# Whole-array matmuls at the end, a selector normalise for the last groups, and group one's K/Q weights first: a transformer block on one core

## The chip, the cores and the metric

One core of a Trainium2 chip. The metric is device time in microseconds (us) of one execution. A profile gives the span from the first to the last instruction, about 2 us less than the time.

## The reference, cut to what matters

```python
B, S, D, H, F = 1, 2048, 640, 32, 1728          # head size 20
def _A_ref(x, wqkv, wo):
    q, k, v = ...                                # x @ wqkv, 32 heads
    scores = einsum("bhqd,bhkd->bhqk", q, k) * Dh ** -0.5
    return (softmax(scores) @ v).reshape(B, S, D) @ wo
def _B_ref(x, w_gate, w_up, w_down):
    return ((x @ w_gate) * (x @ w_up)) @ w_down
h  = x + _A_ref(layernorm(x), wqkv, wo)
h2 = h + _B_ref(layernorm(h), w_gate, w_up, w_down)
```

## The kernel before

It is a program that schedules itself while it is built: it models the engines, chooses at each step what the matmul engine does next, and emits the instructions in that order. On the chip the order is fixed. Queries are cut into six stages of 512, 512, 384, 256, 256 and 128 rows; heads into eight groups of four. One *bank* is 128 keys by 512 scores of one head; there are 2048. ScalarE (ACT) takes the exponential of most banks, two or three per instruction; VectorE (DVE) makes about 310 of them with integer arithmetic. Everything else (projections, output product, layer norm, gate, up, down) is background between the score matmuls, and the background of the last two stages runs on after the last attention sum.

Names in the profile's lines: A and m are banks of scores (m serves background products too), E their exponentials, acc the attention sums, b the banks of background products after the last sum. 128\*32 is a weight tile of 128 rows and 32 columns, and the next pair gives the moving operand.

The parts that the change touches. Background products, as four tiles of 32 columns, so that they run side by side:

```python
    def columns(ps, lhsT, rhs, start, stop, n, width=P):
        for i in range((width + 31) // 32):
            w = min(32, width - 32 * i)
            mm(ps[32 * i:32 * i + w, 0:n], lhsT[:, 32 * i:32 * i + w], rhs, start, stop)
```

The normalise: each head's sum of exponentials is one row of the accumulator. Rows go to memory and back as columns, get a reciprocal, and are broadcast through DRAM:

```python
        free = en.add("DVE", ..., lambda: nc.vector.tensor_copy(a[:, 0:w], bank[:, 0:w]), 0.5)
        e = dma(lambda: nc.sync.dma_start(s_[:, 0:m], a[DH:P:32, 0:w]...), [free])
        e = en.add("DVE", ..., lambda: nc.vector.reciprocal(r_[:, 0:m], s_[:, 0:m]), 1.5)
        e = dma(lambda: nc.sync.dma_start(d[:, 0:w]..., r_[:, 0:m]), [e])
        e = dma(bcast, [e], ...)                                  # b <- d, 32 times each row
        e = en.add("DVE", ..., lambda: nc.vector.tensor_tensor(OnT[g], a, b, ALU.mult), 1)
```

First loads and what group one waits for; when VectorE may take a small bank; when background of a stage may start:

```python
    load_x(0)
    e_qk0 = [None, load_w(D, D + 160)]
    e_qk0[0] = load_w(0, 160)
    ...                                                           # then x1, V, the rest of K, of Q, of V
        ws = ([e_k, e_qk0[1]] if b == 1 else [e_q, e_qk0[0]]) if g == 1 else [e_qk0[b]]
    ...
                    ok = fr and self.late() <= LAG                # LAG = 100
    ...
                    g.since = g.due = a + (b - a) * SPREAD * (i + 1) / len(groups)   # SPREAD = 1.2
```

The softmax here doesn't subtract the row's maximum and nothing guards it: scores larger than these inputs give would overflow.

## Time and profile before

| | before |
|---|---|
| time, median of 3 (lowest to highest); a fourth run makes it 885.91 below | 885.79 us (883.98 to 886.77) |
| span of the profiled run | 883.0 us |
| matmul engine / VectorE / ScalarE busy | 832.6 / 754.5 / 804.4 us |
| exponentials from / to | 17.7 / 834.8 us |
| last attention sum starts | 835.62 us, 47.4 us before the end |

The lines behind it stand in the prediction. Read the last two rows of the table as the skeleton: the time is the start of the exponentials, plus their work and their holes, plus what comes after the last sum.

### The profile page before, as it was taken

The page shows a single profiled execution, that of the slowest core. Times are in us where ns is not written, and L with a number is a line of the kernel's source. Part 1 is how long each engine was busy: PE and PEld are TensorE (multiplying, and loading weights), DVE is VectorE, ACT ScalarE, POOL GpSimd, SP SyncE. Part 2 cuts the span into 40 slices and gives each one's busy share as a digit, 9 for nine tenths or more (in the row PEclk, how much of TensorE's full clock was granted, in tenths as well). Part 3 has the DMA queues.
Part 4 walks back from the last instruction along what each step waited for, and adds up shares of the span by engine and source line. Part 5 has one row for each costly group of instructions (what it writes and reads, how often), then busy time and mean ns, then how long its engine had stood idle before and what let it go on. Part 6 is the DMA issues. An engine that isn't in the chain of part 4 may idle for free. (4 is left out here: it accounts for less than half of the span.)

```text
span 883.0 us, 36981 instructions
## 1 busy us (share of the span) xinstructions
PE 832.6 (94%) x16596; PEld 367.6 (42%) x16596; DVE 754.5 (85%) x1608; ACT 804.4 (91%) x780; POOL 20.8 (2%) x32
## 2 busy tenths in 40 slices
PE   6999999999999999999999999999999999999995
PEld 2444342232334322222344433344444445565774
DVE  4654886999899999999999999989989997998652
ACT  3699989999999999999999999999999999998801
POOL 2020000000000000000000000000000000000000
PEclk9999999999999999999999999999999999999999
DMA  6131212212230233211310233161034311274100
GB/s 206 39 102 29 82 56 63 84 40 79 64 89 22 67 96 90 53 41 36 67 38 28 50 79 72 27 146 34 23 90 97 66 26 31 67 154 77 23 16 19
DMA packets 132950, 56.62 MB, mean 64 GB/s; under 512 B 103096, under 2 KB 130744, under 8 KB 132792
## 3 DMA queue, kind: packets, MB, share of 16 engines
q1 hardware_dynamic: 132792, 54.27, 24.5%
q8 instruction: 129, 2.11, 1.0%
q14 instruction: 29, 0.24, 0.1%
HBM read 45.89 MB, written 8.09 MB: 61 GB/s over the span
## 5 line engine op out<-in xcount | busy, mean ns | idle before, releaser
L740 ACT ACTIVATE E<-A 128x1536 bf16<-128x1536 f32 (+1 forms) x758 | 795.4, 1183 | 21.1 <-PE A L429 12.4
L429 PE MATMUL A<-qT,kT 32*128 32x256 bf16 (+3 forms) x3024 | 296.9, 299 | 22.8 <-ACT E L740 18.6
L429 PEld LDWEIGHTS <-kT 32*128 32x128 bf16 (+1 forms) x3768 | 101.5, 92 | 256.6 <-issue 216.0
L429 PE MATMUL acc<-E,Vx 128*32 128x256 bf16 (+3 forms) x2808 | 190.1, 304 | 4.7 <-ACT E L740 3.0
L754 DVE TENSOR_SCALAR i<-m 128x512 int16<-128x512 f32 x185 | 125.9, 684 | 11.8 <-PE m L429 10.5
L429 PEld LDWEIGHTS <-Vx 128*32 128x32 bf16 x3328 | 69.5, 95 | 102.5 <-issue 94.0
L784 DVE TENSOR_TENSOR fr<-hl,fr 128x1024 bf16<-128x1024 bf16 x157 | 107.0, 682 | 2.0
L787 DVE TENSOR_TENSOR ED<-i,fr 128x1024 int16<-128x1024 int16 x157 | 106.4, 678 | 1.3
L754 DVE TENSOR_SCALAR i<-A 128x512 int16<-128x512 f32 x128 | 87.7, 685 | 11.4 <-PE A L429 9.5
L429 PE MATMUL m<-lnT,Wr 128*32 128x512 bf16 (+7 forms) x1200 | 74.9, 347 | 2.2 <-DVE lnT L1016 0.8
L429 PE MATMUL m<-qT,kT 32*128 32x256 bf16 (+3 forms) x304 | 71.6, 297 | 0.0
L429 PE MATMUL m<-Wd,hh 128*32 128x320 bf16 (+1 forms) x1456 | 71.0, 301 | 0.2 <-DVE i L754 0.2
L429 PE MATMUL m<-ln2T,wg 128*32 128x512 bf16 (+2 forms) x980 | 70.0, 348 | 0.8 <-DVE i L754 0.8
L429 PE MATMUL m<-ln2T,wu 128*32 128x512 bf16 (+2 forms) x980 | 68.7, 348 | 1.3 <-DVE i L754 1.3
L429 PE MATMUL acc<-zt 128*32 128x512 bf16 (+3 forms) x992 | 67.2, 341 | 0.0
L781 DVE TENSOR_SCALAR hl<-fr 128x1024 bf16<-128x1024 int16 x157 | 65.4, 417 | 1.5
L778 DVE TENSOR_SCALAR fr<-i 128x1024 int16<-128x1024 int16 x157 | 64.4, 414 | 1.3
L429 PEld LDWEIGHTS <-hh 128*32 128x32 bf16 (+1 forms) x1792 | 42.9, 96 | 25.8 <-issue 16.4
L429 PE MATMUL m<-shared,On 128*32 128x320 bf16 x1024 | 49.0, 301 | 0.1
L1406 DVE TENSOR_TENSOR hh<-gs,m 128x512 bf16<-128x512 bf16 (+3 forms) x66 | 36.0, 545 | 9.4 <-PE m L429 5.0
L1395 DVE CAST gs<-m 128x512 bf16<-128x512 f32 (+5 forms) x62 | 35.1, 567 | 7.0 <-PE m L429 6.3
L429 PEld LDWEIGHTS <-Wr 128*32 128x32 bf16 (+1 forms) x1200 | 27.6, 96 | 27.2 <-issue 18.1
(71 smaller groups left out, 541.4 us busy)
## 6 DMA issues: line engine op xcount, KB each, us to landing
wg<-in_B_w_gate_dram SPq DMA_DIRECT2D x47, 160.0 KB
wu<-in_B_w_up_dram SPq DMA_DIRECT2D x47, 160.0 KB
rb<-rd SPq DMA_DIRECT2D x16, 256.0 KB
kT<-kq SPq DMA_DIRECT2D x24, 128.0 KB
kq<-stg SPq DMA_DIRECT2D x24, 120.0 KB
out_dram<-ot SPq DMA_DIRECT2D x16, 160.0 KB
shared<-in_A_x_dram SPq DMA_DIRECT2D x14, 160.0 KB
Wd<-in_B_w_down_dram SPq DMA_DIRECT2D x13, 160.0 KB
```

What stands on the lines that cost most here:

```text
L429: nc.tensor.matmul(out_, lhsT=lhsT, rhs=rhs, start=start, stop=stop)
L740: apart(readers, nc.scalar.activation(E[:, 0:size, :], src[:, 0:size, :], ACT.Exp, scale=LN2_ / UNIT))
L754: apart(readers, nc.vector.tensor_scalar(it[:, pos, :], bank.ap, BIAS, 0.0, ALU.add, ALU.max))
L778: nc.vector.tensor_scalar(f[:, 0:n, :], it[:, 0:n, :], 127, None, ALU.bitwise_and)
L781: nc.vector.tensor_scalar(h[:, 0:n, :], f[:, 0:n, :], QR, QK, ALU.subtract, ALU.mult)
L784: nc.vector.tensor_tensor(fb[:, 0:n, :], h[:, 0:n, :], f[:, 0:n, :], ALU.mult)
L787: nc.vector.tensor_tensor(e16[:, 0:n, :], it[:, 0:n, :], fb[:, 0:n, :], ALU.add)
L1395: r = en.add("DVE", dve_ns(w), [e, was], lambda: nc.vector.tensor_copy(gs[0:M, 0:w], ps[0:M, 0:w]), 1)
L1406: r = en.add("DVE", dve_ns(w), [e, ce, was], lambda: nc.vector.tensor_tensor(hh[0:M, 0:w], gs[0:M, 0:w], ps[0:M, 0:w], ALU.mult), 1)
```

## The change

Its intent: fill the hole in the exponentials near 30 us; shorten the end with fewer, wider matmuls; and take the memory round trip out of the last normalises. New scheduling constants came with it.

```diff
+QK0 = 2 * HP * DH + PADR                       # 172 columns
-    e_qk0 = [None, load_w(D, D + 160)]
-    e_qk0[0] = load_w(0, 160)
+    e_qk0 = [None, load_w(D, D + QK0)]
+    e_qk0[0] = load_w(0, QK0)
-        ws = ([e_k, e_qk0[1]] if b == 1 else [e_q, e_qk0[0]]) if g == 1 else [e_qk0[b]]
+        ws = [e_qk0[b]]
@@ whole-array steps once attention is done
+    def shape(self):
+        return "F" if self.att.done() else "C"
     def columns(ps, lhsT, rhs, start, stop, n, width=P):
+        if pe.mode == "F":
+            mm(ps[0:width, 0:n], lhsT[:, 0:width], rhs, start, stop)
+            return
@@ selector normalise (the last group of stage 4, the last two of stage 5)
+        if g >= G - FAST.get(p, 0):
+            spread(p, g, free, a, b, spots)
+            return free
+    def spread(p, g, free, a, b, spots):
+        ...  # matmul of a with a 0/1 selector puts each head's sum on its 32 rows,
+        ...  # then b = reciprocal(ps), OnT[g] = a * b
@@ constants
+LNP = (1.2, 1.2, 1.2, 1.2, 0, 0)
+WP = (1, 1, 1, 1, 0, 0)                        # priorities: stage 4 now like stage 5
-SPREAD = 1.2
+SPREAD = (1.0, 1.0, 0.9, 0.8)
-LAG = 100
+M_END = 1800
-                    ok = fr and self.late() <= LAG
+                    ok = fr and self.flat < M_END
```

(Cut: the same choice of shape in transposes and filler matmuls, the making of the selector, arguments passed along.)

More of the change, by code (lines that the diff above doesn't have):

```diff
@@ L46 @@
 RES = 5
+FAST_LAST = 2
+FAST_PREV = 1
+LNP = (1.2, 1.2, 1.2, 1.2, 0, 0)
+WP = (1, 1, 1, 1, 0, 0)
 INF = float("inf")
@@ L255, in act @@
             last = g.at == len(g.steps) - 1
-            self.charge(s, dur, "C", dur * 2.4, deps, [g.ev] if last else [])
+            self.charge(s, dur, self.shape(), dur * 2.4, deps, [g.ev] if last else [])
             fn(g.bank.ap, g.at == 0, g.at == len(g.steps) - 1)
@@ L270, in next @@
             if known([self.zeros]) <= t and sum(w for x, w in self.recent if x > t - TICK) < ENOUGH:
-                need = FILL + SWITCH + (SWITCH if self.mode != "C" else 0.0)
+                need = FILL + SWITCH + (SWITCH if self.mode != self.shape() else 0.0)
                 if t + need <= max(latest, s) + 20.0 and t < INF:
@@ L287, in fill @@
         n = bank.shape[1]
-        self.charge(s, n / 2.4 + 3.0, "C", float(n), deps, [])
+        self.charge(s, n / 2.4 + 3.0, self.shape(), float(n), deps, [])
         self.filler(bank, new)
@@ L388 @@
     kap4 = keep.tile([P, HP], F32, name="kap4")
+    sel = keep.tile([P, P], F32, name="sel")
     kT = tiles(keep, G, [P, S], BF16, "kT")
@@ L866, in filler @@
         for i in range(HP):
+            if pe.mode == "F":
+                mm(bank, zt[:, 0:P], zt[:, 0:bank.shape[1]], new, new)
+                break
             mm(bank[32 * i:32 * i + 32, :], zt[:, 0:32], zt[:, 0:bank.shape[1]], new, new)
@@ L880 @@
     wo_done = {}
+    FAST = {LASTP: FAST_LAST, LASTP - 1: FAST_PREV}
     def normalise(p, g, ev):
@@ L916, in normalise, with evac, step @@
         return free
+    def spread(p, g, free, a, b, spots):
+        w = WIDTHS[p]
+        def evac(ps, e):
+            r = en.add("DVE", dve_ns(6.5 * w), [e], lambda: nc.vector.reciprocal(b[:, 0:w], ps[:, 0:w]), 0)
+            q = en.add("DVE", dve_ns(w), [r, Later(lambda: wo_done.get(p - 1))], lambda: nc.vector.tensor_tensor(
+                OnT[g][:, 0:w], a[:, 0:w], b[:, 0:w], ALU.mult), 0)
+            for x in spots:
+                rb_free[x] = q
+            on_ev[p, g] = q
+            return r
+        def step(ps, first, last):
+            columns(ps, sel, a[:, 0:w], first, last, w)
+        for x in spots:
+            rb_free[x] = Ev()
+        pe.groups.insert(0, Group([free, e_sel], [(4 * pe_ns(w), step, [])], evac, f"N{p}{g}"))
+        if g == (G - 1 if p < LASTP else 3):
+            stages.append(p)
     stages = []
@@ L1005, in fn @@
                 pt = ps.bitcast(BF16)
+                if pe.mode == "F":
+                    nc.tensor.transpose(pt[:, c * P:(c + 1) * P], src[:, c * P:(c + 1) * P], ident[:])
+                    return
                 for i in range(4):
@@ L1046, in load_w @@
     def load_w(a, b, after=None):
-        n = (b - a) * D * 2 * (2 if b - a <= 160 else 1)
+        n = (b - a) * D * 2 * (2 if b - a <= QK0 else 1)
         fn = lambda: nc.sync.dma_start(Wr[:, :, a:b], wv[:, :, a:b])
@@ L1064, with one_row @@
     e_kap = en.add("DVE", 80.0, [e_kap], lambda: nc.vector.tensor_reduce(kap[:], kap4[:], mybir.AxisListType.X, ALU.add), 0)
+    e_sel = en.add("POOL", 200.0, [], lambda: nc.gpsimd.memset(sel[:], 1.0), 4)
+    for slope in (1, -1):
+        def one_row(slope=slope):
+            view = sel[:].rearrange("p (h e) -> p h e", e=32)
+            nc.gpsimd.affine_select(out=view, in_=view, compare_op=ALU.is_ge, fill=0.0, base=-slope * DH,
+                                    pattern=[[-32 * slope, HP], [0, 32]], channel_multiplier=slope)
+        e_sel = en.add("POOL", 300.0, [e_sel], one_row, 4)
     e_half = en.add("POOL", 100.0, [], lambda: nc.gpsimd.memset(half[:], 0.5), 0)
@@ L1074 @@
     e_v0 = load_w(2 * D, 2 * D + HD)
-    e_k = load_w(D + 160, 2 * D)
-    e_q = load_w(160, D)
+    e_k = load_w(D + QK0, 2 * D)
+    e_q = load_w(QK0, D)
     e_v1 = load_w(2 * D + HD, 3 * D)
@@ L1338, in evac @@
                     r = en.add("DVE", dve_ns(HD), [e, ex], lambda: nc.vector.tensor_tensor(
-                        hr[:, hsl], ps[:, 0:HD], hr[:, hsl], ALU.add), 1 if not last else 0)
+                        hr[:, hsl], ps[:, 0:HD], hr[:, hsl], ALU.add), WP[p])
                     hv[hf].t2 = r
@@ L1355, in second_stage @@
             evs = layer_norm([hrow[hn(i)] for i in idx], [Max(hev[i]) for i in idx], outs,
-                             [fr.get(("ln", i % 2)) for i in idx], 1.2 if not last else 0)
+                             [fr.get(("ln", i % 2)) for i in idx], LNP[p])
             for i, e in zip(idx, evs):
@@ L1446, in more @@
                 for i, g in enumerate(groups):
-                    g.since = g.due = a + (b - a) * SPREAD * (i + 1) / len(groups)
+                    g.since = g.due = a + (b - a) * SPREAD[p] * (i + 1) / len(groups)
             pe.groups += groups
```

## The prediction

> **What bounds the kernel now.** I read the page's busy shares first, then the busy time by stretches, then the two places that stood out: the opening (in order of time) and the end (chain of waits, then in order of time).
>
> ```profile
> PE 832.6 (94%) x16596; PEld 367.6 (42%) x16596; DVE 754.5 (85%) x1608; ACT 804.4 (91%) x780; POOL 20.8 (2%) x32
> ...
> L740 ACT ACTIVATE E<-A 128x1024 bf16<-128x1024 f32 x539 | 529.5, 1061 | 10.4 <-PE A L429 9.8 <-PE m L429 0.3
> L740 ACT ACTIVATE E<-A 128x1536 bf16<-128x1536 f32 x219 | 325.1, 1485 | 10.7 <-PE m L429 6.7 <-PE A L429 2.6 <-PE acc L429 1.1
> ```
>
> ScalarE does nothing but attention exponentials, 539×2 + 219×3 = 1735 banks of 512 columns; the other 313 of 2048 banks go to VectorE in five instructions each pair.
>
> ```profile
> 20.00:30.00 10.00, 9.80 (x163) 4.13 (x158) 3.46 (x13) 6.27 (x7) 1.01 (x1) 1.00 0.04 5
> 30.00:40.00 10.00, 9.62 (x230) 4.87 (x233) 6.03 (x15) 5.28 (x6) 0.00 (x0) 1.00 0.24 77
> ...
> 200.00:300.00 100.00, 95.28 (x1544) 36.13 (x1542) 92.92 (x199) 100.00 (x99) 1.43 (x2) 1.00 0.22 60
> ...
> 860.00:870.00 10.00, 6.18 (x402) 5.66 (x401) 2.84 (x10) 2.13 (x8) 0.00 (x0) 1.00 0.07 21
> ```
>
> Columns are PE, weight loads, DVE, ACT. From 200 to 700 us ACT is full: there only its work counts. So three terms set the time: how early the exponentials run without a hole, how much of them ACT has, and what is left after the last one (834.8 us). The hole in the opening:
>
> ```profile
> 28.00 1.25 PE L429 MATMUL m<-lnT,Wr 128*32 128x512 bf16 x20
> ...
> 29.31 0.59 ACT L1154 CAST kT<-m 128x512 bf16<-128x512 f32 x1 [0.73 <-PE m L429]
> ...
> 34.72 15.70 ACT L740 ACTIVATE E<-A 128x1024 bf16<-128x1024 f32 x17 [4.83 <-PE A L429]
> ```
>
> Head group one's K projection runs only at 28.00 and its Q later, because their weights ride in the big loads; the eight exponentials of group zero are over at 28.6 and ACT has 6.1 us with 0.59 us of work. The end:
>
> ```profile
> 861.61 1.22 PE b L429 x86
> 862.83 1.57 issue
> 864.40 0.40 PE b L429 x14
> 864.80 0.56 PE m L429 x40
> 865.36 1.01 PE b L429 x74
> 866.37 1.51 issue
> 867.87 0.85 PE b L429 x46
> ...
> 869.84 1.51 issue
> 871.36 2.96 PE b L429 x128
> 874.31 0.80 issue
> ```
>
> Between the stalls stand exactly 128 matmuls (14+40+74), 256 instructions with their weight loads. With one more at 845.74 (1.04 us) they cost 6.43 us in which PE waited for nothing visible. Also there, the normalise of the very last group goes through memory and back:
>
> ```profile
> 836.08 0.29 DVE L896 COPY accS<-acc 128x128 f32<-128x128 f32 x1
> ...
> 842.79 0.54 SPq L903 DMA_DIRECT2D rb<-rd  x1
> ...
> 849.41 0.28 DVE L909 TENSOR_TENSOR On<-accS,rb 128x128 bf16<-128x128 f32 x1
> 850.97 2.02 PEld L429 LDWEIGHTS <-On 128*32 128x32 bf16 x64
> ```
>
> 13.6 us from sums to quotient; the last stage's first product starts at 850.97.
>
> **What the Trainium skill says.** "Runtime: NRT & Kernel Launch", section Instruction fetch mechanics: an engine's instructions come through a FIFO refilled in blocks of 256, and crossing a block is mostly hidden. The trace agrees on 256 and disagrees on hidden: with 128-column matmuls one block lasts 1.97 us of work (864.40 to 866.37) and the next comes 3.47 us after the last. "TensorE: Matmul & The Clock Gate", section Back-to-back issue gap, gives about 81 ns for a pair of weight load and 128-column matmul, against about 56 ns without the load; here four 32-column tiles of 128 columns take 0.56 us per ten, 56 ns, with 4×32 weight columns loaded behind them, and 256 columns take 1.09/10 = 109 ns. No 128x128 weight load is in this trace. "TensorEngine Tiling (Array Packing)", section Restrictions, says column tiling disables fast weight load, so whole tiles should not load slower than now; no line shows it yet.
>
> **The change part by part.** I compared the instruction order of both kernels on every engine; counts below are from there, durations from the rows named.
>
> *First weights.* The first K and Q loads widen from 160 to 172 columns and then hold all of group one. Its two projections move ahead of the value projections, with exponentials 9 to 16 no longer behind the large loads. Removed: the hole of 6.1−0.6 = 5.5 us. Added: 40 matmuls of 512 columns earlier, at the opening's slow rate (40 in 4.46 us), replacing 16 filler matmuls: some 2.5 us in front of exponentials that were PE-paced anyway (1.6 us apart, 1.02 us long), part of it hidden. The next gate, the second chunk's layer norm, was ready about 31 us and its K projection about 36, just when exponential 17 will be due. Net −4.5 us, between −2 and −6.
>
> *Scheduling constants.* VectorE banks drop from 313 to 303: the order shows 118 instead of 128 taken from ACT's own tiles and only one from the small banks after bank 1800. ACT then runs 530 of two banks, 228 of three, one of one. By the row at 34.72 a two-bank one costs 15.70/17 = 0.924 us; with 795.4 us busy in all (page, group one), a three-bank one is (795.4−539×0.924)/219 = 1.36 us. After: 530×0.924+228×1.36+0.5 = 800 us, +4.4 us on the bounding engine. Against it: after 34.72 ACT idles 800.1−787.4 = 12.7 us, 5 of them after 750, where the waits name PE's small banks (m) most, which VectorE now leaves alone late. I take −2 us back, 0 to −6.
>
> *Whole-array matmuls after the last attention sum.* The stages after 835.9 have 103 steps of 256 columns, 56+28 of 320, 16 of 320 for the output projection and 145 of 128 with the transposes; the order has nearly the same steps (102) left, so no work moves. Instructions there fall to a quarter, about 840 of 3300: at 3.47 us per 256 this is 11.4 us of fetching for over 30 us of work, so the 6.4 us of stalls go. PE from 835.84 to 879.37 is 43.5 us; less 6.4 leaves 37.1. If weight loads show at 128 columns, 145 steps cost up to 81−56 = 25 ns more, 3.6 us; I take 10 ns, 1.5 us, 0.5 us for the wider ones. A new wait for the last gate-times-up results before the down projection may cost 1 us, as the fetch stalls hid it until now. Net −4 us, 0 to −7.
>
> *Selector normalise.* Three groups (last of the next-to-last stage, two of the last) replace three transfers by one f32 matmul and a full-width reciprocal. From rows of 242 ns at 16 columns and 167 at 4, a column costs 6.25 ns: about 0.94 us at 128, 1.74 at 256. The quotient comes some 3 us after the last sum instead of 13.6. But PE had work meanwhile (840 to 850: 8.96 of 10 busy) and only 0.95 us near 859.65 waited for the last stage's norm. Worth 1 us at most directly; call it −0.5 and the slack that lets whole-array steps follow each other. VectorE sheds 10 banks at 0.685 + (0.683+0.679+0.418+0.415)/2 = 1.78 us, far more than the 3.6 us of reciprocals.
>
> Sum: −4.5 + 4.4 − 2 − 4 − 0.5 = −6.6 us. I add −1.5 us because the parts' favourable sides are longer (the idle time of ACT in the middle is open to repair), giving 885.8 − 8.1, about 877.7 us, 0.9% less.
>
> **Rivals.** First, that the whole-array loads do not hide: each of about 320 steps then adds some 53 ns of load, 17 us, and the stage loses 10 instead of gaining 4; the time would be about 892. Against: column-tiled steps already load 128 columns per 56 ns unseen, and row-tiled loads of 128 columns start 12 ns apart. For: all of them go to different parts of the array, a whole one does not. Second, that ACT's 10 more banks eat the opening's gain and the idle time stays: −0.1 from both together, and 881 remains from the tail. Third, that the opening's hole only moves, to the wait for the second chunk's projections, as PE is 98% busy between 20 and 30: gain 1 us, about 881. Fourth, everything works: −6, +4.4, −6, −7, −1, about 870. For it: the idle time of ACT after 750 has one kind of cause.
>
> **Range and chances.** 870 to 884 covers the fourth rival and both mild ones, not the first. Over 2% faster means below 868.1, more than all favourable ends together: 0.06. Over 2% slower needs 903, beyond even the first rival: 0.01. Within 2%: 0.93.
>
> **What would show it.** Opening: group one's K copy on ACT right after its first exponential, no 4.83 us wait, the 17th exponential near 37 instead of 42. Middle: ACT busy about 4 us more; the last attention sum between 829 and 836. End: no issue stalls of 1.5 us in the chain, steps of 128 columns at 56 to 81 ns and of 256 at about 109 (more than 130 would mean that loads show and I am wrong there), the last quotient 3 us after its sum, and about 42 us instead of 47 from last sum to end. If the last sum comes earlier than 829, I have mis-sized the scheduling constants; if later than 836, the second or third rival holds.

## The result and the profile after

877.17 us (median of 4, 876.99 to 879.09) against 885.91: ratio 0.991, 95% interval 0.989 to 0.993. A ratio here is the mean time of one kernel's fast runs over that of the other's fast runs of the same rounds, so it is not quite the ratio of the medians.

The page and the exponentials of the kernel after:

```profile
PE 832.1 (95%) x15633; PEld 369.9 (42%) x15633; DVE 738.0 (84%) x1578; ACT 808.1 (92%) x781; POOL 21.0 (2%) x35
...
L753 ACT ACTIVATE E<-A 128x1024 bf16<-128x1024 f32 x530 | 526.7, 1074 | 14.7 <-PE A L439 13.9 <-ACT E L753 0.3
L753 ACT ACTIVATE E<-A 128x1536 bf16<-128x1536 f32 x228 | 341.9, 1500 | 3.4 <-PE A L439 2.5 <-PE acc L439 0.3 <-ACT E L753 0.2
```

ScalarE is busy 3.7 us more; 4.4 were worked out from the order. The opening of the kernel after, in order of time:

```profile
24.62 8.55 ACT L753 ACTIVATE E<-A 128x1024 bf16<-128x1024 f32 x9 [0.27 <-PE A L439]
34.60 11.11 ACT L753 ACTIVATE E<-A 128x1024 bf16<-128x1024 f32 x12 [1.42 <-PE A L439]
...
53.60 6.65 ACT L753 ACTIVATE E<-A 128x1024 bf16<-128x1024 f32 x7 [2.70 <-PE A L439]
...
115.97 7.38 ACT L753 ACTIVATE E<-A 128x1024 bf16<-128x1024 f32 x7 [4.10 <-PE A L439]
```

The 4.83 us hole is gone and the 17th exponential starts at 34.60, where it was near 42 before (34.72 plus eight at 0.924). But new waits for scores stand at 53.60 and 115.97. Busy time by stretches, before:

```profile
45.00:100.00 55.00, 54.10 (x1113) 23.20 (x1105) 29.59 (x76) 52.21 (x56) 5.37 (x2) 1.00 0.25 67
100.00:140.00 40.00, 38.88 (x646) 16.15 (x646) 37.11 (x75) 36.17 (x35) 0.00 (x0) 1.00 0.21 64
```

and after (columns: PE, weight loads, DVE, ACT, POOL):

```profile
45.00:100.00 55.00, 53.31 (x1133) 23.66 (x1135) 28.64 (x70) 49.61 (x52) 5.37 (x2) 1.00 0.25 65
100.00:140.00 40.00, 37.75 (x643) 15.96 (x639) 26.22 (x51) 34.42 (x33) 0.00 (x0) 1.00 0.25 75
```

From 45 to 140 us ScalarE does 4.4 us less and VectorE 11.8 us less than before. I counted the banks whose exponential has started by a time (instructions started in the trace, times the banks of each in the order):

| banks begun by | 45 us | 100 us | 140 us | 200 us | 700 us |
|---|---|---|---|---|---|
| before | 40 | 159 | 253 | 409 | 1718 |
| after | 56 | 167 | 252 | 407 | 1717 |

The lead of 16 banks is spent by 140 us. The last attention sum starts at 834.40, only 1.2 us earlier than before, and 0.9 us of that is a first exponential at 16.77 instead of 17.70. The rest of the gain is in the end, which shrinks from 47.4 to 40.7 us:

```profile
834.85 0.29 DVE L914 COPY accS<-acc 128x128 f32<-128x128 f32 x1
...
835.50 0.39 PE L439 MATMUL b<-accS,sel 128*128 128x128 f32 x2
...
836.12 0.95 DVE L944 RECIPROCAL rb<-b 128x128 f32<-128x128 f32 x1
...
837.26 0.28 DVE L945 TENSOR_TENSOR On<-accS,rb 128x128 bf16<-128x128 f32 x1
...
837.91 1.25 PE L439 MATMUL m<-shared,On 128*128 128x320 bf16 x8
...
859.86 1.00 PE L439 MATMUL b<-ln2T,qT 128*128 128x128 bf16 x15
...
860.70 0.44 PE L439 MATMUL m<-ln2T,qT 128*128 128x128 bf16 x5
```

The quotient is there 2.7 us after the copy of its sum (13.6 before). Fifteen whole-array steps of 128 columns take 860.70 − 859.86 = 0.84 us, 56 ns each, the pace of the column tiles; those of 256 take 109 ns (15 from 835.73 to 837.37). No line of the matmul engine after the last sum waits on "issue" for longer than 0.3 us.

So the total came out as predicted while its parts did not: the opening brought no gain that lasted, and the end brought more. The experiments take the parts one by one.

### The profile page after: what moved, and what is told of

It reads as the page before. It is cut to its first block, busy times and chain, and to the rows that moved or that the text cites. A ratio compares the mean times of both kernels' runs of the same rounds, so it can differ in the third digit from the quotient of the medians.

```text
span 875.1 us, 35020 instructions
## 1 busy us (share of the span) xinstructions
PE 832.1 (95%) x15633; PEld 369.9 (42%) x15633; DVE 738.0 (84%) x1578; ACT 808.1 (92%) x781; POOL 21.0 (2%) x35
## 4 chain that ended last, share of the span: by engine, by line
ACT 46%; PE 36%; DVE 13%; issue 4%; DMA 0%; DVEq 0%; ACTq 0%
ACT E L753 46%; PE m L439 16%; PE A L439 10%; PE acc L439 7%; DVE i L767 4%; PE b L439 3%; DVE fr L797 1%; DVE ED L800 1%; DVE fr L791 1%; DVE hl L794 1%; PE m L1052 1%; DVE gs L1448 1%; DVE hh L1459 1%; DVE accS L914 0%; DVE st L1024 0%
## 5 line engine op out<-in xcount | busy, mean ns | idle before, releaser
L797 DVE TENSOR_TENSOR fr<-hl,fr 128x1024 bf16<-128x1024 bf16 (+1 forms) x152 | 103.7, 682 | 1.6
L800 DVE TENSOR_TENSOR ED<-i,fr 128x1024 int16<-128x1024 int16 (+1 forms) x152 | 103.2, 679 | 1.2
L767 DVE TENSOR_SCALAR i<-A 128x512 int16<-128x512 f32 x118 | 81.0, 687 | 12.7 <-PE A L439 10.0
L439 PE MATMUL m<-Wd,hh 128*32 128x320 bf16 (+1 forms) x1484 | 77.3, 301 | 0.1
L439 PE MATMUL acc<-zt 128*32 128x512 bf16 (+3 forms) x1028 | 72.3, 353 | 0.0
L794 DVE TENSOR_SCALAR hl<-fr 128x1024 bf16<-128x1024 int16 (+1 forms) x152 | 63.7, 419 | 1.3
L791 DVE TENSOR_SCALAR fr<-i 128x1024 int16<-128x1024 int16 (+1 forms) x152 | 62.1, 416 | 0.7
L439 PEld LDWEIGHTS <-hh 128*32 128x32 bf16 (+2 forms) x1540 | 41.9, 96 | 26.9 <-issue 15.1
L439 PE MATMUL m<-shared,On 128*32 128x320 bf16 (+1 forms) x968 | 47.6, 301 | 1.2 <-DVE i L767 0.8
L1459 DVE TENSOR_TENSOR hh<-gs,m 128x512 bf16<-128x512 bf16 (+4 forms) x68 | 36.9, 542 | 6.6 <-PE m L439 3.1
```

The costliest lines, as they stand in the source:

```text
L439: nc.tensor.matmul(out_, lhsT=lhsT, rhs=rhs, start=start, stop=stop)
L767: apart(readers, nc.vector.tensor_scalar(it[:, pos, :], bank.ap, BIAS, 0.0, ALU.add, ALU.max))
L791: nc.vector.tensor_scalar(f[:, 0:n, :], it[:, 0:n, :], 127, None, ALU.bitwise_and)
L794: nc.vector.tensor_scalar(h[:, 0:n, :], f[:, 0:n, :], QR, QK, ALU.subtract, ALU.mult)
L797: nc.vector.tensor_tensor(fb[:, 0:n, :], h[:, 0:n, :], f[:, 0:n, :], ALU.mult)
L800: nc.vector.tensor_tensor(e16[:, 0:n, :], it[:, 0:n, :], fb[:, 0:n, :], ALU.add)
```

## The experiments

The change has four parts: *first* (wider first loads), *whole* (whole-array steps after the last sum), *norm* (selector normalise), *const* (constants). Undoing all four in the changed kernel gives the order of the kernel before on PE, ACT, DVE and the DMA queue, instruction for instruction, so they are complete (the trace of half late below, in which all four are undone, agrees for ACT, DVE and the DMA queue). All results below were correct. Every kernel is within 2% of the kernel before, so what is said rests on the 95% intervals. "Left" is the number of 256-column steps after the last sum, in the order; ten of them are half as wide (64 columns) and count as one each. The prediction and the expectations divide the matmuls of column-tiled kernels by four, so their numbers for these (103, 98, 76, 66) are five lower than here.

| kernel | median us | ratio to before (95%) | last sum starts | end after it | left | banks on DVE |
|---|---|---|---|---|---|---|
| before | 885.8 | | 835.6 | 47.4 | 108 | 313 |
| changed | 877.2 | 0.991 (0.989 to 0.993) | 834.4 | 40.7 | 102 | 303 |
| whole only | 879.2 | 0.992 (0.990 to 0.995) | 834.1 | 40.5 | 108 | 313 |
| first only | 888.4 | 1.002 (1.000 to 1.005) | 843.0 | 46.0 | 103 | 310 |
| norm only | 885.5 | 0.999 (0.997 to 1.001) | 841.0 | 42.7 | 81 | 310 |
| const only | 881.0 | 0.994 (0.991 to 0.997) | 835.8 | 45.3 | 71 | 310 |
| changed without first | 875.0 | 0.987 (0.984 to 0.991) | 835.8 | 34.3 | 57 | 310 |
| changed without whole | 880.8 | 0.995 (0.992 to 0.998) | 833.5 | 45.9 | 102 | 303 |
| changed without norm | 878.1 | 0.992 (0.989 to 0.994) | 837.3 | 40.3 | 107 | 303 |

Single executions of one kernel spread over up to 9 us (the kernel before: 880.0 to 889.1), so the two columns from one trace each explain, and the ratios decide.

### One part alone

**whole only** (edit: first, norm and const undone).

> The kernel before with only the whole-array steps after the last attention sum. Everything up to the last sum is the same order of instructions, so the last exponential should end at 834.8 us again, within 1. If the gain of the end is instruction fetch (the four or five stalls of 1 to 1.6 us, 6.4 us in all, gone because the instructions fall to a quarter), the end from last sum to finish shrinks from 47.2 to about 41 and the time to about 880, ratio 0.993. If instead the end is bound by the down projection waiting for the last group's normalise (still through memory here), it stays above 45 and the ratio above 0.997.

Measured 879.2, ratio 0.992: 7 us. Every stall after the last sum is gone, and the end is 6.9 us shorter. That is the fetch theory's number. Two lines of this kernel's trace tell of something else, both in the stretch whose order is that of the kernel before:

```profile
29.49 17.53 ACT L753 ACTIVATE E<-A 128x1024 bf16<-128x1024 f32 x19 [4.92 <-PE A L439]
...
828.78 0.83 PE L439 MATMUL m<-ln2T,qT 128*32 128x256 bf16 x22 [2.02 <-issue]
```

The ninth exponential starts 5.2 us earlier than before (34.72) in the same order: the first 40 projection matmuls took 3.39 us here against 4.46, and twelve filler matmuls 0.83 against 1.47. The clock record in the trace separates the two: the TensorE clock is full, for over 800 us on end, from 13.76 us here and from 27.74 us in the kernel before (it has no record before that, and the stretches view then prints 1.00). In traces with the narrow first loads the ninth exponential comes the later the later that is: full from 13.76, 21.82, 27.74 and 31.07 us, ninth at 29.49, 31.72, 34.72 and 36.14. One order thus has different openings from execution to execution. This lead stays: 10 banks at 140 us, 17 at 700. Part of it is then lost to issue stalls before the last sum: 5.1 us after 60 us, against 2.3 in the kernel before (here 1.12, 1.04 and 2.02 us, between 802 and 829).

**first only** (edit: whole, norm and const undone).

> The kernel before with only the wider first K and Q loads. The order gives ACT 548 exponentials of two banks and 214 of three, 1.5 us more by the estimate, and about 98 steps of 256 columns left after the last sum instead of 103. If the opening's gain survives (exponential 17 at 35 to 37 us instead of 42), the time falls by 4 to 6, ratio 0.993 to 0.996. If it is given back in later waits of ACT for K (the second rival form: the hole only moves), exponential 17 is as early but the last exponential ends within 1.5 us of 834.8 and the ratio is over 0.997.

Measured 888.4, ratio 1.002, so slower if anything. Exponential 17 starts at 34.43, so the hole is filled as intended; waits of 2.70 us at 53.4 and 4.11 us at 115.8 follow at the same places as in the changed kernel (and once more in a second trace of that, below). ACT's idle time between its first and last exponential is 25.9 us, before 21.1. The form of the second rival came true. The last sum is 7.4 us later in the trace, but that is the slowest of six executions (891.0) beside a fast one of the kernel before (884.0); the means differ by 2 us. Nor is the gain in the opening all due to the loads: beside whole only, whose narrow loads also met a full clock early (13.76 us; 16.60 here), exponential 17 comes 2.3 us earlier (36.73, 34.43), not 7.

**norm only** (edit: first, whole and const undone).

> The kernel before with only the selector normalise for the three last groups, everything still column-tiled. The order moves: 76 instead of 103 steps of 256 columns are left after the last sum, ACT has 1.4 us more. If the normalise itself is worth nothing but lets work of the next-to-last stage start before the last sum, the end shrinks by 27 x 0.109 = 3 us and the net is about -1.5, ratio 0.998; if the fetch stalls rule the end (instructions per us), it shrinks by the share of instructions removed, 216 of 3300 at 13.6 ns, 3 us too. If the last stage had waited for the quotient, up to 6 us, ratio 0.993.

Ratio 0.999: nothing. Fewer steps are left at the end (81), and the last sum is later in this trace, behind an issue stall of 3.06 us at 809.5.

**const only** (edit: first, whole and norm undone).

> The kernel before with only the scheduling constants (where background work may start, which banks VectorE may take late, priorities of the next-to-last stage). ACT has 1.3 us more, 66 steps of 256 columns are left at the end instead of 103: 4 us less of PE work there. If the constants are what pays for the ten VectorE banks, net -2 to -4, ratio 0.996 to 0.998. If the work was only moved in front of the exponentials and makes ACT wait there, ratio 1.000 or above.

881.0, ratio 0.994: 5 us, better than the best expected. The order gives ACT only three banks more, not ten, its idle time falls from 21.1 to 19.3 us, and 37 fewer steps are left at the end. These steps are 4 us of work, and the fetch stalls after the last sum fell from 6.4 to 3.3 us, but the end is only 2.1 us shorter. With less work to cover it, the slow normalise now shows: its quotient is there at 849.3, and products, sums and layer norm lead from it to a wait of 2.04 us. After that wait the clock is at half for 3.4 us, and ten steps of 128 columns take 1.06 us there, 106 ns each instead of 56. Waits for gate times up grow too, from 0.42 to 1.79 us. Matmul engine in order of time, then busy time by stretches (the 0.50 is the granted clock):

```profile
857.03 0.46 PE L1052 MATMUL b<-ident,l 128*32 128x128 bf16 x20 [2.04 <-DVE l L1036]
863.94 0.29 PE L439 MATMUL b<-ln2T,qT 128*32 128x128 bf16 x6 [0.92 <-issue]
867.97 0.46 PE L439 MATMUL b<-ln2T,qT 128*32 128x128 bf16 x18 [2.05 <-issue]
...
857.47:860.88 3.41, 3.41 (x96) 2.51 (x88) 0.78 (x2) 0.40 (x2) 0.00 (x0) 0.50 0.00 0
```

So the fast normalise, worthless alone, may be what lets a shorter end be short: the changed kernel without first (57 steps left, below) has no such wait. No run took the normalise out of that kernel, so this is not shown.

### One part taken away

**without first** (edit: the first loads and `ws` as before).

> The changed kernel without the wider first loads. The wider loads alone made the kernel before slower (888.4, +2), although exponential 17 came 7 us earlier, so my part of -4.5 us is in doubt. The order here leaves 57 steps of 256 columns after the last sum (102 in the changed kernel) and ACT has 3 us less to do. If the loads' gain is given back in the middle whatever else is changed, this kernel is faster than the changed one by 2 to 5 us, 872 to 875, ratio to before 0.984 to 0.988. If they pay only together with the new constants, it is slower, 880 to 882, ratio 0.994 to 0.996.

875.0, ratio 0.987, the lower end of the range that meant "given back whatever else is changed". The traces of this kernel and of the changed one have their first exponential at the same 16.77 us, so they compare directly: with the wide loads the last sum is 1.4 us earlier (834.4, 835.8), but 45 more steps of 256 columns are left after it, 4.9 us at 109 ns, and the end is 6.4 us longer.

**without whole** (edit: `shape` always "C").

> The changed kernel with column-tiled steps to the end. The order up to the last sum is the same. If whole-array steps are worth the fetch stalls, these come back: four or more of 1 to 2 us in the stages after the last sum, the end grows from 40.8 to 46 or 47 and the time to 882.5 to 884, ratio 0.996 to 0.998. If something else shortened the end (the normalise, the constants), it grows by less than 3.

880.8; the end is 5.2 us longer, and the stalls are back:

```profile
861.89 0.90 PE L439 MATMUL b<-ln2T,qT 128*32 128x128 bf16 x50 [1.38 <-issue]
865.92 0.23 PE L439 MATMUL b<-ln2T,qT 128*32 128x128 bf16 x2 [2.06 <-issue]
869.68 1.00 PE L439 MATMUL b<-Wd,hh 128*32 128x320 bf16 x24 [1.04 <-issue]
```

Their 4.5 us are most of the 5.2. The time is 1.7 us below what I expected.

**without norm** (edit: `FAST_LAST = FAST_PREV = 0`).

> The changed kernel with all normalises through memory. 107 steps of 256 columns are left after the last sum, 11.7 us of PE work, against 13.6 us from sum to quotient before. If the normalise is off the path, the time stays within 1 us of the changed kernel, 876 to 878.5. If with whole-array steps the last stage's products run into the quotient, PE waits 2 us or more once for it, 879 to 881, ratio 0.992 to 0.994.

878.1: off the path here. 107 steps are left to cover it, and after the last sum its trace has the same two short waits as the changed kernel's (0.59 and 0.28 us).

### Is it the number of instructions?

**half**: in the changed kernel, a whole-array step becomes two tiles of 64 columns.

```diff
         if pe.mode == "F":
-            mm(ps[0:width, 0:n], lhsT[:, 0:width], rhs, start, stop)
+            for i in range((width + 63) // 64):
+                w = min(64, width - 64 * i)
+                mm(ps[64 * i:64 * i + w, 0:n], lhsT[:, 64 * i:64 * i + w], rhs, start, stop)
             return
```

> The changed kernel with the whole-array steps cut into two tiles of 64 columns: the same columns, twice the instructions (about 1680 after the last sum, against 840 and, column-tiled by 32, 3300). If instruction fetch is what counted (256 instructions per 3.5 us), 1680 need 23 us, less than the 36 us of work: no stall, and the time is that of the changed kernel within 1 us. If the tiling itself costs (tiles switching or loads not overlapping), the end grows by about half of what 32-wide tiles cost, 3 us.

876.5, ratio 0.989 (0.986 to 0.992), the end 40.6 us: the changed kernel's. Ten tiles do what five whole steps did, in the same 0.28 us:

```profile
859.05 0.45 PE L439 MATMUL m<-ln2T,qT 128*64 128x128 bf16 x10
859.33 0.72 PE L439 MATMUL b<-ln2T,qT 128*64 128x128 bf16 x20
```

The shape does not matter; halving the instructions is enough. That agrees with a supply of 256 instructions per 3.5 us, 13.6 ns each, against 14 ns wanted here (four instructions per 56 ns) and 7 ns wanted by the 32-wide tiles. (By the trace it is 673 matmuls after the last sum, so 1346 instructions and not 1680; the argument stays.)

The kept traces hold the fetch itself, which the experiments left to inference. The page of the kernel before lists the instruction transfers:

```profile
q8 instruction: 129, 2.11, 1.0%
```

Each moves 16384 bytes, and 129 times 256 is 33,024, where the matmul engine has 33,192 instructions (after: 122 transfers, 31,232 and 31,266). Beside the stalls of the prediction's chain:

| transfer ends | engine idle ("issue") | goes on after the transfer's end by |
|---|---|---|
| 863.15 | 862.83 to 864.40 | 1.25 us |
| 866.40 | 866.37 to 867.87 | 1.47 us |
| 869.99 | 869.84 to 871.36 | 1.36 us |
| 873.74 | 874.31 to 875.11 | 1.37 us |

In all 14 traces, each of the 57 issue stalls over 0.15 us after 60 us ends 1.1 to 1.6 us after such a transfer has landed, and no transfer starts less than 3.29 us after the one before it. After the last sum of the changed kernel three are made, at 837.0, 853.2 and 864.6. So the stalls are waits for instructions.

### Then fewer instructions earlier, too?

**half late**: in the kernel before, background steps are two 64-wide tiles from bank 1500 on (`b = 64 if att.flat >= 1500 else 32`). ACT's and DVE's orders are those of the kernel before.

> The kernel before, the same order on every engine, but from attention bank 1500 of 2048 on all background steps (projections, gate, up, down) are two 64-wide tiles instead of four 32-wide ones: 1800 matmuls and 1800 weight loads fewer. Fetch theory: the stalls of 0.5 to 2 us without a visible cause between 780 and 835 us go as well as those after the last sum, ACT's idle time after 700 us falls from 4.6 to about 2, the end to 41 or 42, the time to 876 to 878, ratio 0.988 to 0.991. Rival: steps of 64-wide tiles among 32-wide attention sums cost a drain at each change of tiling; then ACT idles more after 700 us than before and the time is above that of the whole-array part alone (879.2, ratio 0.992).

883.9, ratio 0.999 (0.996 to 1.002): the rival. All issue stalls after 60 us are gone and the end is 40.3 us, but the attention takes back what the end gives. One stretch before that has no stall in either kernel, before:

```profile
700.00:760.00 60.00, 59.22 (x1370) 30.29 (x1366) 53.43 (x118) 59.96 (x59) 1.06 (x1) 1.00 0.10 28
```

and half late:

```profile
700.00:760.00 60.00, 59.52 (x952) 26.86 (x953) 51.58 (x112) 58.07 (x55) 1.07 (x1) 1.00 0.10 27
```

418 fewer matmuls, no less busy time of PE, four exponentials fewer. From the wait that both have (122.47 before, 119.47 here) to the last sum this kernel takes 6.8 us more. Its order has 120 changes between 64-wide and 32-wide tiles that were none before: about 57 ns each, net of the 2.3 us of stalls that went. The trace prices a change directly. Two steps of 32-wide sums take 0.22 us up to the next sums, and 0.33 us up to a 64-wide step (matmul engine of half late, in order of time):

```profile
724.80 0.40 PE L439 MATMUL acc<-E,Vx 128*32 128x256 bf16 x8
725.02 0.39 PE L439 MATMUL acc<-ED,Vx 128*32 128x256 bf16 x8
725.35 0.72 PE L439 MATMUL m<-Wd,hh 128*64 128x320 bf16 x6
```

Where steps of 256 columns follow each other between 600 and 833 us without a wait, the next one starts a median of 206 to 214 ns after the start of the last across a change (21 places), and 109 to 120 ns without one. At about 0.1 us each, 120 changes are 12 us of the matmul engine, enough for the loss.

**half late on the best** (the same in the changed kernel without first).

> The changed kernel without the wider first loads and with 64-wide background steps from bank 1500 on, whole array after the last sum. If few stalls are left there (1.1 us in that kernel's trace), it gains 1 us at most over it: 873.5 to 875, ratio 0.985 to 0.987. If changing tiling costs, it is slower than it, above 877.

879.8, ratio 0.994 (0.991 to 0.997), in the same rounds as the last one below (871.6). Again no stall is left (the other trace has 3.1 us of them), the end is the same 34.3 us, and the last sum is 5.4 us later with the same opening; 116 changes, 47 ns each net. So it pays only where no 32-wide work is in between.

### Repeats side by side

> The changed kernel again, to stand beside the next one on the same chip: 876.5 to 878, ratio 0.989 to 0.991. Its trace is to show whether exponential 17 comes again near 34 us and the waits at 53 and 116 us are the same: if they are, they are made by the order, not by chance.

877.0, ratio 0.992. Exponential 17 at 33.87, waits of 2.70 us at 52.88 and 4.11 us at 115.26, 252 banks at 140 us: the give-back is made by the order, not by chance. (At 140 us all six traces with the wide loads have 249 to 252 banks; the eight with the narrow ones have 248 to 263, depending on when the clock was full.)

> The changed kernel without the wider first loads again: 874 to 876 and 1.5 to 3 us below the changed kernel of the same rounds, if the loads cost in combination too. Equal within 1 us: then they are neutral in combination, and only their effect alone (+2) stands.

871.6 (869.1 to 876.4), ratio 0.987 (0.984 to 0.990). Means of the same rounds: 872.7 against 877.5, 0.5% less than the changed kernel (4.8 us, give or take 3.3 at 95%). The changed kernel without the wider first loads is the best of all tried, 1.3% below the kernel before.

## Why the prediction was right

877.7 was forecast and 877.2 measured, but three of its four terms were mis-sized and cancelled. That the total came out so near is luck, the −1.5 us added at the end included. Nor do the parts add up: measured alone, they make about −11 us by the ratios, and together −8.

*First weights: −4.5 forecast.* The removal was seen rightly (exponential 17 even earlier than "near 37"). The step that failed is that a hole removed from ACT early stays removed. The third rival named the cause, a matmul engine that is 98% busy in the opening, but placed the limit at the second chunk near 36 us; the traces show it at the waits near 53 and 116 us, and by 140 us the lead was zero. Measured: +2 alone, and +3 to +5 in combination (ratios 0.991 against 0.987; 877.5 against 872.7 us in the same rounds), there as work left over to the end.

*Constants: +4.4 −2 forecast.* Failed where "the order shows" ten banks fewer on VectorE: I charged all ten banks lost by VectorE to the constants. Alone they cost three; so does the normalise, so do the wide loads, and the ten come with the wide loads and the constants together (the changed kernel without first loses three, without norm ten). And "no work moves", read from 103 and 102 steps left (108 and 102 on one count), held only for the sum: the constants take 37 steps away from the end, and without the wide loads the changed kernel leaves 57. Measured alone: −5.

*Whole-array: −4 forecast, within 0 to −7.* Mechanism right, size off. Alone 7 us, without it in the changed kernel about 3.5 us by the ratios and 5.2 us by the end's length. The terms that should reduce it did not appear: the steps of 128 columns cost 56 ns, not 66, and the wait for the last gate-times-up product, set at 1 us more, was 0.28 us (0.42 before). The first rival (weight loads that show) fell. The counts of about 840 and 3300 instructions were too high: after the last sum the traces have 349 and 1372 matmuls, so with their loads about 700 and 2740.

*Selector normalise: −0.5 forecast.* Right: 0.999 alone, and without it the changed kernel has 0.992 instead of 0.991. The part of it that "lets whole-array steps follow each other" is not shown in that form; what is shown is the 2.04 us wait in const only, where the end was short and the normalise slow.

A small slip: VectorE takes six instructions for a pair of banks, not five (313 first ones and four times 157 on the page).

What stays open: which of the four constants carries the gain (and const was never taken away from the changed kernel); why exactly the scheduler, given earlier scores, leaves 45 more steps to the end; what the normalise is worth where few steps are left; and whether the changes of tiling are the whole cost of the 64-wide steps in the attention.

## What to carry to other kernels

Filling an early hole of the bounding engine is worth only what is still there some stages later: count finished units at fixed times in both traces, and look what is left after the last one. Where stalls have no visible cause, count the instructions between them and look at the instruction transfers; if the count is a constant, make fewer instructions rather than faster ones, but not by mixing tile widths. And when one order replaces another, price the parts by building each alone: counts taken from the sum of all parts can be charged to the wrong one. Before two traces are compared by their openings, look from when on each had the full clock.

## What the Trainium skill lacked or had wrong

- "Runtime: NRT & Kernel Launch", section Instruction fetch mechanics: that crossing a block of 256 instructions is mostly hidden does not hold for streams of small matmuls. Here one block arrived per about 3.5 us, column-tiled steps of 128 columns used one up in 2 us, and stalls of 0.9 to 2.1 us returned with the 32-wide tiles. The page gives no rate of supply; here no transfer of a block started less than 3.29 us after the one before it.
- "TensorE: Matmul & The Clock Gate", section Back-to-back issue gap: about 81 ns for a weight load with a 128-column matmul is too much for this case: 128x128 loads with 128 columns ran at 56 ns a pair.
- "TensorEngine Tiling (Array Packing)", section Key Properties: that a change of tiling mode drains the engine is stated without a cost. Here a change between 32- and 64-wide tiles put off the next step of 256 columns by about 0.1 us, and about 120 added changes came with 5.4 to 6.8 us.
